# Scores of the first eight head pairs from whole fp32 operands, reads in natural order by TensorE, an earlier first load, and a re-fitted order

## The chip, the cores and the metric

One core of a Trainium2 chip runs the whole program: TensorE (PE, with its weight loads PEld), VectorE (DVE), ScalarE (ACT), GpSimd (POOL), and SyncE (SP), on whose queue all loads and stores of this kernel are issued. The metric is the device time of one execution in microseconds, the median of the runs.

## The reference, cut to what matters

```
q, k, v: (8, 12, 448, 64) fp32        w_in (768, 1024), w_spatial (448, 448), w_out (512, 768): float64
s    = cap * tanh(q k^T / sqrt(64) / cap)
attn = exp(s - max) / (sum(exp(s - max)) + 1e-9)
x    = attn v, heads side by side                  # (8, 448, 768)
h    = relu(x w_in); u, v = halves of h            # 512 columns each
v_n  = layernorm of v over its columns
out  = (u * (w_spatial v_n + b_spatial)) w_out     # (8, 448, 768)
```

The first four lines are called attention here, the rest the feed-forward part.

## The kernel before, in words

**Work units.** The 96 heads are worked in 48 pairs, six to a batch. A pair's keys are cut into four blocks of 112, worked two at a time (j = 0 and 1). For each j there is a score group on TensorE (into two buffers `ps_s`, one per block), two tanh on ScalarE (L545, reading `ps_s`, writing half of a tile `tp`), one exp over all of `tp` (L550), and a group of four matmuls that multiplies `tp` by the values (L559, into `ps_x`). Scores are transposed: keys lie on partitions, queries run along the free dimension. There are four `tp` tiles and two `ps_s` buffers, so j = 1 of a pair can't fill `ps_s` before the tanh of j = 0 has read it.

**Two precisions of matmul.** A matmul on plain fp32 operands (the values' group, and `ones` below) appears in the trace as two instructions. The scores are done in another way: `raw` (one buffer; 448 query and 448 key columns of both heads, one head on partitions 0 to 63, the other on 64 to 127) is rounded by ScalarE to `qh` (L310), VectorE subtracts to get the rest `ql` (L306), both in the type fp32r, and three terms qh·qh, ql·qh, qh·ql are accumulated: twelve single instructions for each j, which run in pairs (one head in each half of the array).

**Denominators.** The softmax's maximum is taken after exp. For each pair VectorE takes the larger of the two `tp` tiles (L580 over 1792 elements, L580 over 896), transposes blocks of 32 (L585), and reduces (L587) into `st`; a round trip through DRAM (`md`, `dt`) brings the partial results onto 32 partitions, where L616, L624 and L626 make the reciprocals, which go out (`rd`) and come back spread over the partitions (`rr`). The sum is taken by the same four VectorE instructions, except for the first `PE_SUMS` = 10 pairs: there TensorE multiplies `tp` by a block of ones (L599, eight matmuls in four column groups), ScalarE copies the rows to `sx` (L602), and DMAs bring them back (`td`, `dt`). POOL then multiplies (L645) and the result is split in two for the feed-forward part (`xg`).

**Natural order.** The host stores the queries permuted, query i·14+b at column b·32+i, because that is what the 32-blocks of the VectorE transpose want. Before the change the copies out of PSUM undo it: L564 and L602 read `ps_x` and `ps_acc` in a row and write with a step of 14 elements.

**Feed-forward part.** For each batch: u chains (L678 to L680), v chains (L700 to L705, whose rows are normalised by VectorE and POOL), gate chains (L769 to L774), output chains (L794 to L796), all in fp32r with three terms, chained in PSUM tiles `ps_acc`. Batch b's feed-forward matmuls are mixed with the next batch's pairs; the last batch's stand alone at the end. The weights come as float64 bits and are turned into `wi_h`, `wi_l` (12 pieces) and `wo_h`, `wo_l` (12 smaller pieces) once, in the first 180 us: POOL (L375), three VectorE operations (L379, L380, L382), a ScalarE cast, a VectorE subtraction (`wi_l`, L306).

**Order.** A planner (`Plan.order`) simulates the engines with a cost for each task and at each moment gives an engine the ready task with the smallest key. The keys come from `BND_KEY` and `BND_W_KEYS`; `TURN` and `STICK` are what it charges when TensorE changes between kinds of matmul, `MM`, `MMW` and `FF` its costs of matmuls. So these numbers change no instruction, only the order.

**Start.** Ahead of everything, `cap` is loaded and its bits decide a branch: here the `bounded` side is taken. Fourteen bf16 matmuls on zeros (`warm`) run while that is going on.

Of the kernel before, what the change touches and what calls it, by code (L numbers as in the profile page):

```python
# [167 lines left out]
HW, HH, XL, XF = 475, 650, 50, 4 / 360  # L170

# [68 lines left out]
def attn_moe(ctx, tc, bounded, shared, qk, v, qk2, v2, cap, w_in, w_sp, w_out, out):  # L240
# [278 lines left out]
    def pair_bnd(b, hp, xf, rr):  # L519
# [5 lines left out]
        t0 = add("S", HW, kk("ld"), lambda: nc.sync.dma_start(out=raw.t, in_=qk2[b, hp]), allocs=[raw], lat=XF * 128 * PW)  # L525
# [3 lines left out]
        t0 = add(e0, ct(e0, PW), kk("hi"), lambda: copy(e0, qh.t, raw.t), [t0], [raw], [qh], name="qh")  # L529
        t2 = add(e1, st2(e1, PW), kk("hi"), lambda: sub(e1, ql.t, raw.t, f(qh.t)), [t0], [raw, qh], [ql], name="ql")  # L530
        x, tps, exps, prev = Buf("x"), [], [], None
        for j in range(2):
            ps, tp = [Buf("s"), Buf("s")], Buf("tp")

            def scores(j=j, ps=ps):
                for i in range(2):
                    for n, (y, z) in enumerate(((qh, qh), (ql, qh), (qh, ql))):
                        for e in range(2):
                            r, c = slice(e * D, (e + 1) * D), S + (2 * j + i) * KB
                            nc.tensor.matmul(ps[i].t[:KB, e, :S], lhsT=y.t[r, c:c + KB], rhs=z.t[r, :S], start=(n == 0), stop=(n == 2))  # L540

            s = add("T", 6 * MM, kk("sc", j), scores, [t0, t2], [qh, ql, *ps], ps, name="sc", mode="R")
            for i in range(2):
                th = add("A", act(PW, 1), kk("th", j),
                         lambda i=i, ps=ps, tp=tp: nc.scalar.activation(  # L545
                             out=tp.t[:KB, i * PW:(i + 1) * PW].rearrange("p (e q) -> p e q", q=S), in_=ps[i].t[:KB, :, :S],
                             func=AF.Tanh, scale=ic[:KB]),
                         [s], [ps[i], tp], [tp] if i == 0 else [], name="tanh")
            ex = add("A", act_s(2 * PW, 1), kk("ex", j),
                     lambda tp=tp: nc.scalar.activation(out=tp.t[:KB], in_=tp.t[:KB], func=AF.Exp, scale=ca[:KB]), [th], [tp],  # L550
                     name="exp")
            tps.append(tp)
            exps.append(ex)

            def pv(j=j, tp=tp):
                for i in range(2):
                    for e in range(2):
                        c, o = 2 * j + i, (2 * i + e) * S
                        nc.tensor.matmul(x.t[e * D:(e + 1) * D, 0, :S], lhsT=vt.t[:KB, (2 * c + e) * D:(2 * c + e + 1) * D],  # L559
                                         rhs=tp.t[:KB, o:o + S], start=(c == 0), stop=(c == 3))  # L560
# [3 lines left out]
        z = add("A", act(S), kk("ev"), lambda: nc.scalar.copy(  # L564
            out=xf.t.rearrange("p (i b) -> p b i", b=QB), in_=x.t[:, 0, :S].rearrange("p (b i) -> p b i", i=32)), [prev], [x, xf],
            [xf], name="xev")

# [24 lines left out]
        if by_pe:  # L592
            acc, sx, td = Buf("acc"), Buf("sx"), Buf("td")

            def ones():
                for c in range(4):
                    for e in range(2):
                        o, i = e * D + c % 2 * 32, (c % 2 * 2 + e) * S
                        nc.tensor.matmul(acc.t[o:o + 32, 0, :S], lhsT=one[:KB], rhs=tps[c // 2].t[:KB, i:i + S], start=(c < 2), stop=(c > 1))  # L599
# [16 lines left out]
        d0 = add("V", 185, kk("dn"), lambda: nc.vector.reduce_max(  # L616
            out=sec(0), in_=grp()[:, :, :2 * QB].rearrange("p g b -> p b g"), axis=AX.X), [d], [dt], name="mred2")
# [201 lines left out]
def either(ctx: ExitStack, tc: tile.TileContext, *args):  # L819
# [5 lines left out]
    nc.sync.dma_start(out=capt[:, 0:1], in_=args[4].broadcast_to([128, 1]))
    with tc.tile_pool(name="wps", bufs=1, space=bass.MemoryType.PSUM) as wp, tc.tile_pool(name="warm", bufs=1) as ww:
        warm = ww.tile([128, WARM_N], mybir.dt.bfloat16, name="warm")
        nc.vector.memset(warm, 0.0)
# [2 lines left out]
            nc.tensor.matmul(ps, lhsT=warm[:, :128], rhs=warm, start=True, stop=True)  # L831
# [6 lines left out]
    nc.vector.memset(half, -0.5)  # L838
# [33 lines left out]
```

## Time and profile before

| | us |
|---|---|
| runs shown | 802.78 (median), 802.62, 805.45 |
| the profiled execution, its own time | 804.6 |
| its span, first to last instruction | 802.7 |
| PE / DVE / ACT / POOL busy | 763.1 / 707.3 / 575.5 / 228.6 |

A group's row gives, after the bar, busy time in us, the mean of one instruction in ns, and then the idle time of its engine just ahead of such instructions with what ended it. Busy time of PE counts a matmul up to its modelled end, so the distance from one start to the next, as the list in order of time shows it, is what a matmul costs in a stream.

### The profile page before, as it was taken

Reading aid. Unit: us, or ns where it says so; the run is one execution under the profiler, and the core shown is the slowest. Engines: PE = TensorE matmul, PEld = TensorE weight load, DVE = VectorE, ACT = ScalarE, POOL = GpSimd, SP = SyncE. Lnnn points to the kernel's source line nnn. Section 1 sums busy time; section 2 is a strip of 40 time slices with the busy share of each in tenths; the row PEclk is TensorE's granted clock in tenths of the full one; section 3 lists DMA queues with packets and bytes.
Section 4 is the critical chain, followed back from the end, with each engine's and each line's share of the span. In section 5 each row is a group of like instructions: output and inputs, shape, how many; then the busy total and the mean of one; then the engine's idle time right before and its main releaser. Section 6 shows DMA issues by size and latency. Waiting matters only on the chain.

```text
span 802.7 us, 11490 instructions
## 1 busy us (share of the span) xinstructions
PE 763.1 (95%) x4126; PEld 528.4 (66%) x4126; DVE 707.3 (88%) x934; ACT 575.5 (72%) x699; POOL 228.6 (28%) x179
## 2 busy tenths in 40 slices
PE   6878899979999999999999999999999999999997
PEld 2333456646776766667667677767677766767796
DVE  4979997899899997999999999999999999999340
ACT  4999877595777867687678876887677876874131
POOL 3131133341242103440143313330244212431150
PEclk8999999999999999999999999999999999999999
DMA  5544532433222332124221332223221332112102
GB/s 176 182 109 125 152 111 62 125 89 121 60 61 74 97 112 58 48 62 131 75 61 50 120 97 61 69 68 113 93 59 51 107 99 68 54 52 73 38 1 73
DMA packets 51254, 69.04 MB, mean 86 GB/s; under 512 B 23754, under 2 KB 36596, under 8 KB 51188
## 3 DMA queue, kind: packets, MB, share of 16 engines
q1 hardware_dynamic: 51188, 68.22, 28.7%
q8 instruction: 34, 0.56, 0.3%
q14 instruction: 32, 0.26, 0.1%
HBM read 55.70 MB, written 12.49 MB: 85 GB/s over the span
## 4 chain that ended last, share of the span: by engine, by line
PE 54%; DVE 24%; DMA 8%; ACT 7%; issue 5%; POOL 1%; SPq 1%; ACTq 0%; DVEq 0%; POOLq 0%
PE ps_x L559 10%; DVE red L580 10%; PE ps_s L540 9%; PE ps_acc L678 4%; PE ps_acc L679 4%; PE ps_acc L680 4%; DVE red L585 3%; DVE st L587 3%; ACT tp L545 2%; DMA dt<-md 2%; PE ps_acc L772 2%; ACT tp L550 2%; PE ps_acc L774 2%; PE ps_acc L773 2%; PE ps_acc L794 2%
## 5 line engine op out<-in xcount | busy, mean ns | idle before, releaser
L545 ACT ACTIVATE tp<-ps_s,capt 112x896 f32<-112x896 f32 x192 | 184.6, 1005 | 9.9 <-PE ps_s L540 8.9
L580 DVE TENSOR_TENSOR red<-tp 112x1792 f32<-112x1792 f32 x86 | 180.6, 2110 | 10.0 <-ACT tp L550 10.0
L550 ACT ACTIVATE tp<-tp,capt 112x1792 f32<-112x1792 f32 x96 | 172.4, 1796 | 2.3
L645 POOL TENSOR_TENSOR xf<-xf,rr 128x448 f32<-128x448 f32 x48 | 86.2, 1797 | 280.1 <-DMA rr<-rd 267.6
L559 PE MATMUL ps_x<-tp,v 112*64 112x448 f32 x768 | 157.2, 549 | 4.6 <-ACT tp L550 2.7
L559 PEld LDWEIGHTS ps_x<-tp,v 112*64 112x64 f32 x768 | 50.4, 137 | 87.2 <-issue 75.7
L580 DVE TENSOR_TENSOR red<-red 112x896 f32<-112x896 f32 x86 | 103.4, 1203 | 0.5
L585 DVE STREAM_TRANSPOSE red<-red 128x896 f32<-128x896 f32 x86 | 94.0, 1093 | 0.9
L587 DVE TENSOR_REDUCE st<-red 128x28 f32<-128x896 f32 x86 | 90.8, 1077 | 1.1
L540 PE MATMUL ps_s<-qh 64*112 64x448 f32 x384 | 81.2, 417 | 10.2 <-ACT tp L545 6.4
L540 PE MATMUL ps_s<-qh,ql 64*112 64x448 f32 x384 | 72.8, 372 | 6.6 <-DVE ql L306 6.5
L306 POOL TENSOR_TENSOR xg<-o,xg 128x448 fp32r<-128x448 f32 x32 | 46.1, 1443 | 107.4 <-ACT xg L310 107.4
L540 PEld LDWEIGHTS ps_s<-qh 64*112 64x112 f32 x384 | 34.0, 173 | 63.8 <-issue 28.1
L540 PE MATMUL ps_s<-ql,qh 64*112 64x448 f32 x384 | 72.2, 368 | 0.0
L678 PE MATMUL ps_acc<-xg,wi_h 128*128 128x448 f32 x186 | 69.7, 375 | 1.3 <-ACT xg L310 1.2
L794 PE MATMUL ps_acc<-xg,wo_h 128*128 128x448 f32 x184 | 69.3, 376 | 1.5 <-DVE o L779 1.2
L679 PE MATMUL ps_acc<-xg,wi_h 128*128 128x448 f32 x186 | 68.9, 371 | 1.1 <-DVE xg L306 1.1
L795 PE MATMUL ps_acc<-xg,wo_h 128*128 128x448 f32 x184 | 67.4, 366 | 1.6 <-POOL xg L306 1.6
L680 PE MATMUL ps_acc<-xg,wi_l 128*128 128x448 f32 x186 | 68.6, 369 | 0.0
L796 PE MATMUL ps_acc<-xg,wo_l 128*128 128x448 f32 x184 | 67.4, 366 | 0.0
L310 ACT CAST xg<-xf 128x448 fp32r<-128x448 f32 x96 | 36.5, 402 | 34.3 <-POOL xf L645 31.7
L306 DVE TENSOR_TENSOR ql<-raw,qh 128x896 fp32r<-128x896 f32 x48 | 53.3, 1111 | 7.2 <-ACT qh L310 7.2
(123 smaller groups left out, 1386.7 us busy)
## 6 DMA issues: line engine op xcount, KB each, us to landing
raw<-in_qk SPq DMA_DIRECT2D x48, 448.0 KB
v<-in_v SPq DMA_DIRECT2D x48, 224.0 KB
rr<-rd SPq DMA_DIRECT2D x96, 112.0 KB
out<-o SPq DMA_DIRECT2D x48, 224.0 KB
w<-in_w_in SPq DMA_DIRECT2D x12, 512.0 KB
xg<-in_w_out SPq DMA_DIRECT2D x12, 256.0 KB
md<-st SPq DMA_DIRECT2D x38, 28.0 KB
dt<-md SPq DMA_DIRECT2D x38, 28.0 KB
```

The costliest lines, as they stand in the source:

```text
L306: eng[e].tensor_tensor(o, a, b, op=ALU.subtract)
L540: nc.tensor.matmul(ps[i].t[:KB, e, :S], lhsT=y.t[r, c:c + KB], rhs=z.t[r, :S], start=(n == 0), stop=(n == 2))
L545: lambda i=i, ps=ps, tp=tp: nc.scalar.activation(out=tp.t[:KB, i * PW:(i + 1) * PW].rearrange("p (e q) -> p e q", q=S), in_=ps[i].t[:KB, : ...
L550: lambda tp=tp: nc.scalar.activation(out=tp.t[:KB], in_=tp.t[:KB], func=AF.Exp, scale=ca[:KB]), [th], [tp],
L559: nc.tensor.matmul(x.t[e * D:(e + 1) * D, 0, :S], lhsT=vt.t[:KB, (2 * c + e) * D:(2 * c + e + 1) * D], rhs=tp.t[:KB, o:o + S], start=(c == ...
L580: tt = lambda g, o_, i0, i1, op=op: eng[g].tensor_tensor(o_, i0, i1, op=op)
L585: d = add("V", dve(PW), kk(key), lambda r=r: nc.vector.transpose(out=blk(r.t[:, PW:]), in_=blk(r.t[:, :PW])), [d], [r], name="vtr")
L587: done.append(add("V", dve(PW), kk(key), lambda r=r, a=a, red=red: red(out=st.t[:, 2 * a * QB:2 * (a + 1) * QB], in_=blk(r.t[:, PW:]), axi ...
L645: m = add(E_X[0], st2(E_X[0], 448), k, lambda: eng[E_X[0]].tensor_tensor(xf.t, xf.t, rr.t, op=ALU.mult), deps, [xf, rr], name="xmul")
L678: nc.tensor.matmul(ps, lhsT=wi_h[:, c, fs], rhs=x[:, XH:], start=(c == 0), stop=False)
L679: nc.tensor.matmul(ps, lhsT=wi_h[:, c, fs], rhs=x[:, :S], start=False, stop=False)
L680: nc.tensor.matmul(ps, lhsT=wi_l[:, c, fs], rhs=x[:, XH:], start=False, stop=(c == NP - 1))
```

## The change

1. **Whole scores.** For the first `WHOLE` = 8 pairs no `qh` and `ql` are made; the scores are plain fp32 matmuls straight from `raw`.
2. **Natural order read by TensorE.** The values' group and `ones` read `tp` through `nat`: consecutive columns are 32 elements apart. The copies L564 and L602 become plain.
3. **First load and table ahead of the branch.** Pair 0's `raw` is a tile of its own (`raw0`, which later pairs use as the one `raw` buffer), loaded right behind `cap`; a tanh on one column makes ScalarE load its function table there too.
4. **Order.** New keys, weights' keys and costs; `PE_SUMS` 10 to 11.

```
-    TURN, STICK = 200.0, 0.74
+    TURN, STICK = 100.0, 0.68
-MM, MMW, TR = 207, 233, 109
+MM, MMW, TR = 204, 227, 109
-BND_KEY = dict(hi=-3.26, ld=-5.98, ...
+BND_KEY = dict(hi=-4.17, ld=-4.9, ...
...
-PE_SUMS = 10
+WHOLE = 8
+PE_SUMS = 11
...
+        if at:
+            t0 = add("S", HW, kk("ld"), lambda: nc.sync.dma_start(out=raw.t, in_=qk2[b, hp]), allocs=[raw], lat=XF * 128 * PW)
+        else:
+            t0 = add("S", 0, kk("ld") - 9, lambda: None, allocs=[raw])
...
+        whole = b * NP + hp < WHOLE
...
+        if not whole:
+            t0 = add(e0, ct(e0, PW), kk("hi"), lambda: copy(e0, qh.t, raw.t), [t0], [raw], [qh], name="qh")
+            t2 = add(e1, st2(e1, PW), kk("hi"), lambda: sub(e1, ql.t, raw.t, f(qh.t)), [t0], [raw, qh], [ql], name="ql")
+        terms = [(raw, raw)] if whole else [(qh, qh), (ql, qh), (qh, ql)]
...
+            if whole:
+                s = add("T", 2 * FF, kk("sc", j), scores, [t0], [raw, *ps], ps, name="sc", mode="R")
...
+            nat = lambda y: y.rearrange("p (b i) -> p i b", i=32)
...
-                                         rhs=tp.t[:KB, o:o + S], start=(c == 0), stop=(c == 3))
+                                         rhs=nat(tp.t[:KB, o:o + S]), start=(c == 0), stop=(c == 3))
...
-        z = add("A", act(S), kk("ev"), lambda: nc.scalar.copy(
-            out=xf.t.rearrange("p (i b) -> p b i", b=QB), in_=x.t[:, 0, :S].rearrange("p (b i) -> p b i", i=32)), [prev], [x, xf],
-            [xf], name="xev")
+        z = add("A", act(S), kk("ev"), lambda: nc.scalar.copy(out=xf.t, in_=x.t[:, 0, :S]), [prev], [x, xf], [xf], name="xev")
...
     nc.sync.dma_start(out=capt[:, 0:1], in_=args[4].broadcast_to([128, 1]))
+    raw0 = const.tile([128, PW], F32, name="raw0")
+    nc.sync.dma_start(out=raw0, in_=args[2][0, 0])
...
+    nc.scalar.activation(out=capt[:, 5:6], in_=half, func=AF.Tanh)
     bits = nc.values_load(capt[0:1, 1:2].bitcast(mybir.dt.int32), min_val=0, max_val=0x7FFFFFFF)
```

**What moves, on two engines.** Lines of the changed kernel are some 5 to 16 higher than before (L545 is L560, L559 is L576, L580 is L595, L306 is L311, L525 is L531).

SP at the start of the program, before (`capt` is cap's tile, `w_...` are pieces of w_in):

```order
L825 DMA capt<-in_cap 128x1
L834 TENSOR_LOAD capt
L840 COMPARE_AND_BRANCH
L525 DMA raw<-in_qk 128x896
L526 DMA v<-in_v 112x512 x2
L368 DMA w_187<-in_w_in 128x1024
L368 DMA w_189<-in_w_in 128x1024
```

and after:

```order
L838 DMA capt<-in_cap 128x1
L840 DMA raw_60<-in_qk 128x896
L851 TENSOR_LOAD capt
L856 COMPARE_AND_BRANCH
L534 DMA v<-in_v 112x512 x2
L373 DMA w_185<-in_w_in 128x1024
L373 DMA w_187<-in_w_in 128x1024
```

The first `raw` stands ahead of the branch, and the weights' loads move up one place.

DVE from the second `ql` of before to the third (`w_...` and `wy` are pieces of w_in on their way, `red_173` the tile of the first pair's reduction), before:

```order
L306 TENSOR_TENSOR ql<-raw,qh 128x896
L382 SCALAR_TENSOR_TENSOR wy<-w_191,wy 128x512
L306 TENSOR_TENSOR wi_l<-wy,wi_h 128x512
L379 TENSOR_SCALAR wy<-wy 128x512
L580 TENSOR_TENSOR red_173<-tp 112x1792
L380 SCALAR_TENSOR_TENSOR wy<-w_240,wy 128x512
L580 TENSOR_TENSOR red_173<-red_173 112x896
L306 TENSOR_TENSOR wi_l<-wy,wi_h 128x512
L585 STREAM_TRANSPOSE red_173<-red_173 128x896
L382 SCALAR_TENSOR_TENSOR wy<-w_240,wy 128x512
L587 TENSOR_REDUCE st<-red_173 128x28
L306 TENSOR_TENSOR ql<-raw,qh 128x896
```

and the stretch that stands there after:

```order
L311 TENSOR_TENSOR wi_l<-wy,wi_h 128x512
L387 SCALAR_TENSOR_TENSOR wy<-w_187,wy 128x512
L595 TENSOR_TENSOR red_173<-tp 112x1792
L311 TENSOR_TENSOR wi_l<-wy,wi_h 128x512
L595 TENSOR_TENSOR red_173<-red_173 112x896
L387 SCALAR_TENSOR_TENSOR wy<-w_195,wy 128x512
L600 STREAM_TRANSPOSE red_173<-red_173 128x896
L342 CAST ws_h<-wy 128x448
L602 TENSOR_REDUCE st<-red_173 128x28
L311 TENSOR_TENSOR wi_l<-wy,wi_h 128x512
L342 CAST ws_h<-wy 128x448
L595 TENSOR_TENSOR red_174<-tp 112x1792
```

No `ql` stands between the weights' pieces and the reductions any more, up to the ninth pair's. The last `wi_l` stands behind eight pairs' reductions (behind nine before), and two pieces of `wo_l` that stood ahead of it are now behind it.

SP around the load of the fifth pair's `raw`, after (`td_453` takes the third pair's sums from `sx`):

```order
L642 DMA rr_406<-rd_390 64x448 x2
L621 DMA dt_410<-td_375 32x2x14 x2
L627 DMA dt_410<-md_368 32x4x28
L534 DMA v_432<-in_v2 112x512
L618 DMA td_453<-sx_448 1x448
L531 DMA raw0_60<-in_qk2 128x896
L618 DMA td_453<-sx_448 1x448 x2
L640 DMA rd_472<-dt_410 32x2x14
```

The load of `raw` stands behind the first of the four DMAs that take the third pair's sums from `sx`; before the change the fifth pair's load stood behind those of the second pair.

More of the change, by code (lines that the diff above doesn't have):

```diff
@@ L216 @@
 BND_TAGS = {
-    "raw": (PW, F32, 1), "qh": (PW, F32R, 1), "sx": (448, F32, 1), "ql": (PW, F32R, 1), "v": (512, F32, 2), "tp": (2 * PW, F32, 4),
+    "qh": (PW, F32R, 1), "sx": (448, F32, 1), "ql": (PW, F32R, 1), "v": (512, F32, 2), "tp": (2 * PW, F32, 4),
     "xf": (448, F32, 2), "rr": (448, F32, 2), "st": (4 * QB, F32, 2), "dt": (20 * QB, F32, 2), **MOE_TAGS, "xg": (XW, F32R, 7),
@@ L224 @@
 ANY_W_KEYS = 2.0, 0.5, 8.0, 9.0, 1.0
-BND_KEY = dict(hi=-3.26, ld=-5.98, vld=-4.91, sc=-1.55, th=-0.93, ex=-1.87, pv=0.89, sm=0.69, mx=1.06, dn=-0.09,
-               ev=3.19, x=2.62, moe=0.79, span=12.63, step=0.24, mv=-1.51)
+BND_KEY = dict(hi=-4.17, ld=-4.9, vld=-1.5, sc=-1.65, th=1.93, ex=-1.09, pv=0.8, sm=0.23, mx=-0.07, dn=-0.32, ev=3.56,
+               x=2.65, moe=0.79, span=12.19, step=0.25, mv=-2.07)
 BND_V_FIRST = 1
 WARM, WARM_N = 14, 512
-BND_W_KEYS = 1.5, 1.89, 7.51, 13.76, 1.19
+BND_W_KEYS = 3.34, 2.17, 7.86, 13.43, 1.08
 E_SUM, E_RED = "VV", "VV"
-PE_SUMS = 10
+WHOLE = 8
+PE_SUMS = 11
 E_W = "PAV"
@@ L268, in make @@
             b.t = reds.pop(0)
+        elif b.tag == "raw" and bounded:
+            b.t = raw0
         elif b.tag == "md":
@@ L274, in make @@
             b.t = dr.tile([2 * S], F32, name="rd")
-    ic, ca, nca, half = shared
+    ic, ca, nca, half, raw0 = shared
     wi_h = const.tile([128, NP, DF], F32R, name="wi_h")
@@ L300, in attn_moe @@
     bufs["red"] = RED
+    if bounded:
+        bufs["raw"] = 1
     plan = Plan(bufs)
@@ L536, in scores @@
                 for i in range(2):
-                    for n, (y, z) in enumerate(((qh, qh), (ql, qh), (qh, ql))):
+                    for n, (y, z) in enumerate(terms):
                         for e in range(2):
                             r, c = slice(e * D, (e + 1) * D), S + (2 * j + i) * KB
-                            nc.tensor.matmul(ps[i].t[:KB, e, :S], lhsT=y.t[r, c:c + KB], rhs=z.t[r, :S], start=(n == 0), stop=(n == 2))
-            s = add("T", 6 * MM, kk("sc", j), scores, [t0, t2], [qh, ql, *ps], ps, name="sc", mode="R")
+                            nc.tensor.matmul(ps[i].t[:KB, e, :S], lhsT=y.t[r, c:c + KB], rhs=z.t[r, :S], start=(n == 0),
+                                             stop=(n == len(terms) - 1))
+            if whole:
+                s = add("T", 2 * FF, kk("sc", j), scores, [t0], [raw, *ps], ps, name="sc", mode="R")
+            else:
+                s = add("T", 6 * MM, kk("sc", j), scores, [t0, t2], [qh, ql, *ps], ps, name="sc", mode="R")
             for i in range(2):
@@ L598, in ones @@
                         o, i = e * D + c % 2 * 32, (c % 2 * 2 + e) * S
-                        nc.tensor.matmul(acc.t[o:o + 32, 0, :S], lhsT=one[:KB], rhs=tps[c // 2].t[:KB, i:i + S], start=(c < 2), stop=(c > 1))
+                        nc.tensor.matmul(acc.t[o:o + 32, 0, :S], lhsT=one[:KB], rhs=nat(tps[c // 2].t[:KB, i:i + S]), start=(c < 2), stop=(c > 1))
             sums = add("T", 2 * FF, kk("pv", 1) + 0.01, ones, exps, [u, w, acc], [acc], name="ones", mode="Q")
-            sums = add("A", 951, kk("ev"), lambda: nc.scalar.copy(
-                out=sx.t.rearrange("p (i b) -> p b i", b=QB), in_=acc.t[:, 0, :S].rearrange("p (b i) -> p b i", i=32)), [sums], [acc, sx],
-                [sx], name="sev")
+            sums = add("A", act(S), kk("ev"), lambda: nc.scalar.copy(out=sx.t, in_=acc.t[:, 0, :S]), [sums], [acc, sx], [sx], name="sev")
             sums = [add("S", HW, kk("dn"), lambda r=r: nc.sync.dma_start(out=td.t[r * S:(r + 1) * S], in_=sx.t[32 * r:32 * r + 1]), [sums],
@@ L823, in either @@
     const = ctx.enter_context(tc.tile_pool(name="shared", bufs=1))
-    capt = const.tile([128, 5], F32, name="capt")
+    capt = const.tile([128, 6], F32, name="capt")
     nc.sync.dma_start(out=capt[:, 0:1], in_=args[4].broadcast_to([128, 1]))
+    raw0 = const.tile([128, PW], F32, name="raw0")
+    nc.sync.dma_start(out=raw0, in_=args[2][0, 0])
     with tc.tile_pool(name="wps", bufs=1, space=bass.MemoryType.PSUM) as wp, tc.tile_pool(name="warm", bufs=1) as ww:
@@ L833, in either @@
     nc.vector.tensor_scalar(ca.bitcast(U32), capt[:, 0:1].bitcast(U32), 0x7FFFFFFF, None, op0=ALU.bitwise_and)
+    nc.vector.memset(half, -0.5)
+    nc.scalar.activation(out=capt[:, 5:6], in_=half, func=AF.Tanh)
     bits = nc.values_load(capt[0:1, 1:2].bitcast(mybir.dt.int32), min_val=0, max_val=0x7FFFFFFF)
@@ L837, in either @@
     nc.vector.tensor_scalar(nca, ca, -1.0, None, op0=ALU.mult)
-    nc.vector.memset(half, -0.5)
-    shared = ic, ca, nca, half
+    shared = ic, ca, nca, half, raw0
     with tc.If(bits <= CAP_BITS) as cmp:
```

13 lines of the change are left out of this document (5 added, 8 removed).

## Prediction

> **What bounds the kernel now.** I read the page's busy shares first, then a table of stretches, then the list in order of time for the start, then the groups.
>
> ```profile
> span 802.7 us, 11490 instructions
> ...
> PE   6878899979999999999999999999999999999997
> DVE  4979997899899997999999999999999999999340
> ACT  4999877595777867687678876887677876874131
> ```
>
> The digits are tenths of a slice of 20 us. After some 200 us PE is at 9 throughout; before that VectorE and ScalarE are the full ones and PE has holes. The stretches show how large these are (PE, PEld, DVE, ACT, POOL busy, then the granted clock).
>
> ```profile
> 0.00:13.00 13.00, 7.67 (x26) 3.45 (x26) 1.88 (x7) 2.85 (x3) 3.43 (x7) 0.83 0.54 159
> 13.00:50.00 37.00, 28.40 (x190) 11.95 (x186) 32.23 (x46) 36.22 (x39) 9.18 (x10) 0.96 0.56 171
> 50.00:85.00 35.00, 29.53 (x201) 13.14 (x199) 32.24 (x44) 32.71 (x35) 6.67 (x7) 0.96 0.40 108
> 85.00:121.30 36.30, 32.07 (x165) 19.17 (x162) 34.82 (x55) 29.83 (x38) 10.20 (x9) 0.95 0.46 137
> ...
> 150.00:180.00 30.00, 24.92 (x144) 16.47 (x142) 28.71 (x53) 21.70 (x32) 13.81 (x15) 1.00 0.42 122
> ...
> 270.00:360.00 90.00, 87.50 (x469) 59.43 (x468) 82.82 (x101) 64.45 (x79) 27.29 (x18) 1.00 0.27 80
> 360.00:451.00 91.00, 90.69 (x495) 65.07 (x494) 88.66 (x109) 70.19 (x85) 26.91 (x19) 1.00 0.27 81
> ```
>
> From 360 us on a batch takes 91 us and PE is busy in 90.69 of them: there only less work on PE would help, and VectorE with 88.66 is close behind. The holes are at the start. Up to 121.3 us PE is busy for 7.67 + 28.40 + 29.53 + 32.07 = 97.7 us, idle for 23.6; VectorE is busy for 101.2, idle for 20.1, of which 11.1 lie in the first 13 us; ScalarE for 101.6, idle for 19.7, with 10.1 in the first 13. I cut at 121.3 because there the last piece of `wi_l` begins. What VectorE does up to there:
>
> ```profile
> L580 DVE TENSOR_TENSOR red<-tp 112x1792 f32<-112x1792 f32 x9 | 18.1, 2014 | 2.9 <-ACT tp L550 2.9
> L306 DVE TENSOR_TENSOR ql<-raw,qh 128x896 fp32r<-128x896 f32 x10 | 10.9, 1091 | 6.3 <-ACT qh L310 6.3
> ...
> L306 DVE TENSOR_TENSOR wi_l<-wy,wi_h 128x512 fp32r<-128x512 f32 x12 | 8.2, 681 | 0.1
> ```
>
> Nine pairs' reductions, ten `ql`, all twelve pieces. From 13 to 121.3 us VectorE is busy for 99.3 of 108.3 us, so the weights come as fast as VectorE gets to them, and TensorE can't fill its holes with feed-forward work before they are there. That is the bound of this stage; ScalarE (98.8 of 108.3) is the next.
>
> **The start.**
>
> ```profile
> 1.17 5.19 PE L831 MATMUL wps<-warm 128*128 128x512 bf16 x14 [1.17 <-DVE capt L838]
> 4.48 0.35 SPq L525 DMA_DIRECT2D raw<-in_qk  x1
> 7.76 1.28 ACT L310 ACT_TABLE_LOAD   x1 [7.76 <-DMA raw<-in_qk]
> 9.06 0.94 ACT L310 CAST qh<-raw 128x896 fp32r<-128x896 f32 x1
> 10.09 0.71 PE L540 MATMUL ps_s<-qh 64*112 64x448 f32 x2 [3.73 <-ACT qh L310]
> 12.37 2.13 ACT L545 ACTIVATE tp<-ps_s,capt 112x896 f32<-112x896 f32 x2 [2.37 <-PE ps_s L540]
> 13.01 0.67 POOL L375 TENSOR_SCALAR wy<-w 128x512 f32<-128x512 f32 x1 [3.22 <-DMA w<-in_w_in]
> ```
>
> The rows give start and duration. `raw` is issued behind the branch at 4.48, the table load and the cast `qh` wait for it, the first score comes at 10.09 and the first tanh at 12.37; POOL's first piece of weights, which waits for its load, at 13.01. After the change `raw` leaves right behind `cap` (in the air while `warm` runs), so scores need only the end of `warm` at 1.17 + 5.19 = 6.36 and the branch: about 7.0 for the first score, some 8.2 for the first tanh, 4 us earlier. But VectorE is the bound, and it begins with weights. Their loads no longer stand behind 448 KB of `raw`. Between 4.48 and 13.01 went, by their shapes, raw with 448, two v with 224 each and w with 512 KB; without raw's share of 8.5 us it would be up to 448/1408 x 8.5 = 2.7 us less, at least 0 if something else sets 13.01. I take 1.5, in the middle. The table load (1.28 us) was on ScalarE's path ahead of `qh`; now it is ahead of the branch, hidden under `warm`.
>
> **Whole scores.** On VectorE eight `ql` go: 8 x 1.091 = 8.7 us, all ahead of the last `wi_l`. (The order puts one of nine reductions and two of the small `wo` pieces behind it; that is work moved, not saved.) On ScalarE eight `qh` go. On TensorE the price is read here:
>
> ```profile
> 21.70 1.72 PE L559 MATMUL ps_x<-tp,v 112*64 112x448 f32 x8 [0.50 <-ACT tp L550]
> 23.35 1.71 PE L599 MATMUL ps_acc<-tp,one 112*32 112x448 f32 x16
> 24.99 0.46 PE L540 MATMUL ps_s<-qh 64*112 64x448 f32 x2
> 25.28 0.37 PE L540 MATMUL ps_s<-qh,ql 64*112 64x448 f32 x2
> 25.49 0.37 PE L540 MATMUL ps_s<-ql,qh 64*112 64x448 f32 x2
> 25.69 0.38 PE L540 MATMUL ps_s<-qh 64*112 64x448 f32 x2
> ```
>
> A values' group of four fp32 matmuls (eight instructions, two abreast) lasts from 21.70 to 23.35: 1.65 us with the change of kind, so 1.50 of streaming in four steps of 0.376. The fp32r terms of the scores start 0.20 apart (25.28, 25.49, 25.69), six steps to a group: 1.20, or 1.29 with its longer first step. A whole group has four fp32 matmuls in the two halves of the array, hence I cost it like the values' group: 1.50, or 0.3 more, x 16 groups = 4.8 us. No row shows fp32 operands in two row halves; if the halves ran one after the other, a group would be 3.0 us, 28.8 us more in all; if they cost like the fp32r terms, nothing. I take 4.8, nearest to the rows for fp32. It falls in the stage in which PE is idle for 23.6 us; with 10.2 us less stage (sum below) 8.6 us of that cover are left.
>
> **Natural order.** The copies get shorter, and the reads of TensorE get steps of 32 elements.
>
> ```profile
> L550 ACT ACTIVATE tp<-tp,capt 112x1792 f32<-112x1792 f32 x96 | 172.4, 1796 | 2.3
> L564 ACT COPY xf<-ps_x 128x448 f32<-128x448 f32 x48 | 46.2, 962 | 8.1 <-DVE xg L306 5.8 <-PE ps_x L559 1.2 <-PE ps_acc L703 0.7
> L310 ACT CAST qh<-raw 128x896 fp32r<-128x896 f32 x48 | 45.6, 950 | 8.1 <-PE ps_s L540 7.6 <-DMA raw<-in_qk 0.4
> L310 ACT COPY o<-ps_acc 128x448 f32<-128x448 f32 x46 | 24.4, 535 | 45.7 <-DMA out<-o 24.3 <-PE ps_acc L796 18.0 <-PE ps_s L540 1.8
> L616 DVE TENSOR_REDUCE dt<-dt 32x28 f32<-32x112 f32 x48 | 16.0, 334 | 8.4 <-DMA dt<-md 8.2
> L587 DVE TENSOR_REDUCE st<-red 128x28 f32<-128x896 f32 x86 | 90.8, 1077 | 1.1
> ```
>
> The copy into `xf`, which writes with a step, took 962 ns (`sx` is of the same form), a plain copy of 128x448 out of PSUM (`o`) 535: 0.43 us less x 59 copies on ScalarE. Together with `qh` that is 8 x 0.95 + 16 x 0.43 = 14.5 us less in the first stage, so ScalarE will not be what holds VectorE up. Later ScalarE is at 3/4 and the gain is only that of waits:
>
> ```profile
> L559 PE MATMUL ps_x<-tp,v 112*64 112x448 f32 x768 | 157.2, 549 | 4.6 <-ACT tp L550 2.7 <-ACT xf L564 1.8
> L540 PE MATMUL ps_s<-qh,ql 64*112 64x448 f32 x384 | 72.8, 372 | 6.6 <-DVE ql L306 6.5
> ```
>
> The first row ends with PE's waits for the copy `xf`, 1.8 us; I take 1.0 (0 to 1.8). The second row's 6.5 us of waits for `ql` end where no `ql` is made.
>
> What strided reads cost TensorE no row shows. There are 96 x 4 + 11 x 4 = 428 fp32 steps that read `tp`. The lower end is 0 (nothing makes a longer step a gain). The upper is the ratio that ScalarE pays, 962/535 = 1.80: 0.30 us a step, 129 us in all. VectorE's strided reduction (334 ns for 112 elements, against 1077 for 896 in a row) says that reads pay, too. Which is nearer? An fp32 step spends 376 ns on 448 columns, 0.84 ns each; an fp32r step 0.45. So an fp32 column already has twice the time of one that TensorE can take at its full rate, while ScalarE and VectorE pay a factor of about two against their own full rate. I take 0. [...]
>
> **One more pair with `ones`.** VectorE loses four instructions, where PE is the bound; PE gets one group: +1.6 (23.35 to 24.99).
>
> **The single `raw` buffer.** TensorE now holds it until the j = 1 scores are done, and the load that follows takes
>
> ```profile
> 11.21 5.39 DMA raw<-in_qk
> ```
>
> 5.39 us among the weights' loads. From the end of one pair's first two tanh, ScalarE has exp, two tanh, exp (1.80 + 2.13 + 1.80, the pair of tanh as at 12.37) and two plain copies with two or three casts, by the rows above an estimated 2.5 us, ahead of the next pair's: 8.2 us. The load's path is about 1.0 for the rest of the scores, 0.35 to issue, 5.39, 0.75 for one block, and 0.4 of hand-overs: 7.9. So it is just hidden, at no cost; each us by which SP issues it late shows.
>
> **The order.** Kinds of matmul change 213 times instead of 218, at about 0.1 us each (25.28 - 24.99 = 0.29 against 0.20): -0.5. In the steady part the groups stand in the same pattern. What the new order can do to the holes at 150 to 180 (5.1 us idle) and 270 to 360 (2.5) is anything from -7.6 to about as much more; I take 0. The planner's changed costs are no instructions.
>
> **The sum.** VectorE's lead at the last `wi_l`: 8.7 + 1.5 = 10.2. From there PE is the bound, and its work is as before but for +1.6, -0.5 and -1.0. So -10.2 + 1.6 - 0.5 - 1.0 = -10.1 us: span 802.7 to 792.6. The profiled execution took 804.6, 1.9 more than its span, and the median of the runs is 802.78, 1.8 below it; on the median I get 792.7, rounded 792.5. Half a per cent, about 4 us, is what a measurement here can tell from no change.
>
> **The rivals.**
> 1. *Strided reads cost TensorE.* For: the ScalarE and VectorE rows above. Against: the fp32 step's slack. [...] At ScalarE's ratio the time is 792.5 + 129 = 921; at a third of that 835. It decides from 10.1/428 = 24 ns a step: beyond that the kernel is slower than before.
> 2. *The load of `raw` becomes the wait.* For: SP has the fifth pair's load behind `td`, which waits for ScalarE's copy `sx`, and ScalarE's own chain has only 0.3 us of slack. Against: fewer bytes before it. If SP's queue holds it for some 1.7 us in each of seven pairs, the 10 us are gone: about 802, no change.
> 3. *Row halves don't run abreast in fp32.* Of 28.8 us instead of 4.8, 24.0 more, 8.6 are covered: 792.5 + 15.4 = 808, slower. Against: fp32r row halves and fp32 column halves both do.
>
> **Chances.** My forecast 0.75, with its own range 780 to 799. Below: the order's -7.6, the loads' further -1.2, the waits' further -0.8, and some 3 of the 9.0 us that VectorE idles from 13 to 121 us. Above: the order's loss, up to where no change begins. Rival 1 0.12, rival 2 0.10, rival 3 0.03. So faster 0.75, within half a per cent 0.10, slower 0.15. The range of 780 to 803 takes in rival 2 and leaves out the slower cases and a little below.
>
> **What would show it.** Right: whole-score groups about 1.5 us apart, values' groups still four steps of 0.376, `xf` copies near 535 ns, first tanh near 8.2 us, the last `wi_l` near 110 or, by the moved work, some 8 us earlier, the steady batches still 91 us, PE idle before 121 us down from 23.6 to about 10. Wrong: values' steps above 0.40 (rival 1), PE or ScalarE waiting for DMA `raw` at each of the first eight pairs (rival 2), whole groups of 3 us (rival 3), or new waits of PE after 150 us.

## The result and the profile after

The changed kernel takes 947.86 us (median, 947.01 to 949.24) against 803.62 for the kernel before on the same chip: a ratio of 1.178, with an interval of 1.175 to 1.181. The profiled execution took 949.24 us, with a span of 947.4. The prediction said 792.5. What was given as its first rival came, at more than its price.

The head of the page after, with the busy shares, the digits of three engines, and the chain that ended last:

```profile
span 947.4 us, 11388 instructions
PE 933.1 (98%) x4078; PEld 532.2 (56%) x4078; DVE 684.8 (72%) x922; ACT 554.5 (59%) x693; POOL 206.8 (22%) x179
...
PE   8998999999999999999999999999999999999997
...
DVE  4677556667977887787877787778787877787540
ACT  4666565566574656665675565846566665746132
...
PE 97%; DMA 2%; DVE 0%; issue 0%; ACT 0%; SPq 0%; POOL 0%; ACTq 0%; DVEq 0%
```

PE's digits are 9 nearly from the first slice to the last, its busy time rose from 763.1 to 933.1 us, and VectorE and ScalarE, full at the start before, now stand at 4 to 7 in the first ten slices. TensorE alone is the bound. The stretches say the same (PE, PEld, DVE, ACT, POOL busy):

```profile
85.00:121.30 36.30, 36.30 (x135) 9.79 (x134) 19.49 (x31) 21.04 (x25) 3.96 (x4) 1.00 0.31 89
...
360.00:451.00 91.00, 91.00 (x414) 55.16 (x413) 72.37 (x90) 55.77 (x68) 20.74 (x17) 1.00 0.22 64
```

In the stretch ahead of 121.3 us, where PE had 4.2 us of holes before, it has none. From 360 to 451 us it is busy as before, but 414 matmuls fit into the stretch where 495 did. The groups that show why (busy time, mean of one, idle time ahead):

```profile
L576 PE MATMUL ps_x<-tp,v 112*64 112x448 f32 x768 | 309.0, 956 | 1.6 <-ACT tp L565 0.8 <-ACT xf L581 0.8
L614 PE MATMUL ps_acc<-tp,one 112*32 112x448 f32 x176 | 43.6, 1093 | 0.0
L551 PE MATMUL ps_s<-raw 64*112 64x448 f32 x128 | 31.3, 610 | 6.5 <-DMA raw<-in_qk 3.7 <-ACT wi_h L315 2.2 <-ACT tp L560 0.4
L581 ACT COPY xf<-ps_x 128x448 f32<-128x448 f32 x48 | 25.5, 532 | 54.5 <-PE ps_x L576 47.2 <-issue 4.8 <-DVE xg L311 2.5
```

L576 is the values' group (L559 before): the same 768 instructions, 309.0 us instead of 157.2. L581, the copy into `xf`, did fall from 962 ns to 532. In order of time, PE:

```profile
20.67 3.25 PE L576 MATMUL ps_x<-tp,v 112*64 112x448 f32 x8
23.85 4.06 PE L614 MATMUL ps_acc<-tp,one 112*32 112x448 f32 x16
27.84 1.76 PE L551 MATMUL ps_s<-raw 64*112 64x448 f32 x8
29.54 3.28 PE L576 MATMUL ps_x<-tp,v 112*64 112x448 f32 x8
```

A values' group of four steps lasts from 20.67 to 23.85, 3.18 us; before it was 1.65 (21.70 to 23.35). A `ones` group takes 3.99 instead of 1.64. The whole scores, which read `raw` in a row, take 1.70, just as costed. So only the two kinds of matmul that read `tp` with a step of 32 elements are dear. (The word has two uses here: a step of so many *elements* is the distance in the tile between two columns read in succession; a values' or `ones` step is the *time* from the start of one instruction, or of those that run abreast, to the next within a group.) Over all groups the median of a values' step is 0.773 us instead of 0.376; a `ones` step takes about 0.99, a quarter of its group. A whole batch now takes 109.5 us from its first values' group to the next batch's, instead of 91.

### The profile page after: what moved, and what is told of

Read it like the earlier page. It is cut to its first block, busy times and chain, and to the rows that moved or that the text cites. A ratio compares the mean times of both kernels' runs of the same rounds, so it can differ in the third digit from the quotient of the medians.

```text
span 947.4 us, 11388 instructions
## 1 busy us (share of the span) xinstructions
PE 933.1 (98%) x4078; PEld 532.2 (56%) x4078; DVE 684.8 (72%) x922; ACT 554.5 (59%) x693; POOL 206.8 (22%) x179
## 4 chain that ended last, share of the span: by engine, by line
PE 97%; DMA 2%; DVE 0%; issue 0%; ACT 0%; SPq 0%; POOL 0%; ACTq 0%; DVEq 0%
PE ps_x L576 32%; PE ps_s L551 15%; PE ps_acc L614 5%; PE ps_acc L807 4%; PE ps_acc L691 4%; PE ps_acc L692 4%; PE ps_acc L693 4%; PE ps_acc L809 4%; PE ps_acc L808 4%; PE ps_acc L716 3%; PE ps_acc L717 3%; PE ps_acc L718 3%; PE ps_acc L785 2%; PE ps_acc L787 2%; PE ps_acc L786 2%; PE ps_acc L713 1%
## 5 line engine op out<-in xcount | busy, mean ns | idle before, releaser
L576 PE MATMUL ps_x<-tp,v 112*64 112x448 f32 x768 | 309.0, 956 | 1.6 <-ACT tp L565 0.8
L560 ACT ACTIVATE tp<-ps_s,capt 112x896 f32<-112x896 f32 x192 | 185.4, 1009 | 65.2 <-PE ps_s L551 64.6
L595 DVE TENSOR_TENSOR red<-tp 112x1792 f32<-112x1792 f32 x85 | 177.1, 2100 | 25.9 <-ACT tp L565 25.6
L576 PEld LDWEIGHTS ps_x<-tp,v 112*64 112x64 f32 x768 | 55.7, 149 | 194.2 <-issue 184.1
L658 POOL TENSOR_TENSOR xf<-xf,rr 128x448 f32<-128x448 f32 x48 | 62.0, 1291 | 351.5 <-DMA rr<-rd 350.1
L595 DVE TENSOR_TENSOR red<-red 112x896 f32<-112x896 f32 x85 | 100.7, 1185 | 0.4
L311 DVE TENSOR_TENSOR ql<-raw,qh 128x896 fp32r<-128x896 f32 x40 | 43.6, 1090 | 76.7 <-ACT qh L315 72.7
L602 DVE TENSOR_REDUCE st<-red 128x28 f32<-128x896 f32 x85 | 91.0, 1070 | 1.0
L315 ACT CAST qh<-raw 128x896 fp32r<-128x896 f32 x40 | 37.8, 946 | 89.4 <-PE ps_s L551 89.4
L311 POOL TENSOR_TENSOR xg<-o,xg 128x448 fp32r<-128x448 f32 x32 | 48.9, 1541 | 156.6 <-ACT xg L315 156.6
L551 PE MATMUL ps_s<-qh 64*112 64x448 f32 x320 | 66.3, 409 | 0.0
L551 PEld LDWEIGHTS ps_s<-qh 64*112 64x112 f32 x320 | 27.9, 170 | 66.0 <-issue 57.4
L551 PE MATMUL ps_s<-ql,qh 64*112 64x448 f32 x320 | 59.2, 362 | 0.0
L551 PE MATMUL ps_s<-qh,ql 64*112 64x448 f32 x320 | 59.0, 362 | 0.0
```

What stands on the lines that cost most here:

```text
L560: lambda i=i, ps=ps, tp=tp: nc.scalar.activation(out=tp.t[:KB, i * PW:(i + 1) * PW].rearrange("p (e q) -> p e q", q=S), in_=ps[i].t[:KB, : ...
L595: tt = lambda g, o_, i0, i1, op=op: eng[g].tensor_tensor(o_, i0, i1, op=op)
```

## The experiments

**E1: the change without the strided reads of TensorE.** The values' group and `ones` read in a row again, ScalarE's two copies write with a step again; each engine's order is that of the changed kernel.

```
-                                         rhs=nat(tp.t[:KB, o:o + S]), start=(c == 0), stop=(c == 3))
+                                         rhs=tp.t[:KB, o:o + S], start=(c == 0), stop=(c == 3))
...
-        z = add("A", act(S), kk("ev"), lambda: nc.scalar.copy(out=xf.t, in_=x.t[:, 0, :S]), [prev], [x, xf], [xf], name="xev")
+        z = add("A", act(S), kk("ev"), lambda: nc.scalar.copy(
+            out=xf.t.rearrange("p (i b) -> p b i", b=QB), in_=x.t[:, 0, :S].rearrange("p (b i) -> p b i", i=32)), [prev], [x, xf],
+            [xf], name="xev")
...
```

> The changed kernel with its natural-order reads alone undone: TensorE reads tp in a row again, ScalarE's copies write with the step again, and every engine's order is that of the changed kernel. If the strided reads cost TensorE everything that was lost (a values' step of 0.773 us against 0.376 over 384 steps is 152 us, and 44 steps of ones at about 1.0 against 0.376 another 27), the time is 948 - 180 + the idle time of PE that comes back, and the rest of the change shows what it is worth: by the forecast 793, between 780 and 803. If the new order or the whole scores cost time too, it ends above 807.

Measured: 790.3 us (789.12 to 792.08), 0.984 of before (0.981 to 0.987). The head of its page, stretches and groups:

```profile
span 788.7 us, 11388 instructions
PE 761.1 (96%) x4078; PEld 524.4 (66%) x4078; DVE 672.7 (85%) x922; ACT 570.8 (72%) x693; POOL 214.1 (27%) x179
...
0.00:13.00 13.00, 9.91 (x38) 3.39 (x38) 0.79 (x6) 6.97 (x7) 3.86 (x8) 1.00 0.63 180
13.00:50.00 37.00, 26.84 (x136) 8.38 (x136) 32.41 (x49) 27.86 (x29) 11.30 (x11) 0.91 0.44 137
50.00:85.00 35.00, 29.95 (x155) 11.02 (x156) 28.87 (x42) 31.78 (x37) 10.13 (x9) 0.90 0.63 181
85.00:121.30 36.30, 35.72 (x188) 21.16 (x187) 30.28 (x50) 27.42 (x34) 9.70 (x8) 1.00 0.30 94
121.30:150.00 28.70, 28.62 (x172) 19.00 (x175) 24.20 (x52) 20.78 (x29) 10.61 (x14) 1.00 0.36 107
150.00:180.00 30.00, 28.69 (x170) 18.72 (x164) 24.67 (x41) 25.45 (x35) 11.40 (x8) 1.00 0.37 115
...
270.00:360.00 90.00, 90.00 (x494) 65.27 (x492) 83.64 (x107) 68.47 (x84) 23.12 (x18) 1.00 0.27 81
...
L576 PE MATMUL ps_x<-tp,v 112*64 112x448 f32 x768 | 159.6, 555 | 2.5 <-ACT xf L581 1.6 <-ACT tp L565 0.8
L616 PE MATMUL ps_acc<-tp,one 112*32 112x448 f32 x176 | 18.8, 545 | 0.0
L551 PE MATMUL ps_s<-raw 64*112 64x448 f32 x128 | 31.3, 608 | 14.7 <-DMA raw<-in_qk 14.2 <-ACT tp L560 0.4
```

One edit moves the span by 947.4 - 788.7 = 158.7 us. Of PE's 172.0 us more busy time (933.1 - 761.1), the values give 149.4 (309.0 - 159.6) and `ones` 24.8 (43.6 - 18.8). PE's idle time went down from 27.6 to 14.3, the 13.3 us between 172.0 and 158.7. So the whole of the loss is the strided reading, and everything else in the change together gains.

**E2: the kernel before with the strided reads alone** (E1's edits the other way, on the kernel before).

> The kernel before with the natural-order reads alone, its own keys and qh, ql for all pairs. If the strided reads are the cause by themselves: 384 steps 0.397 longer and 40 steps 0.62 longer are 177 us more work on PE, of which at most the 20 to 40 us that PE idled before are covered, so 940 to 980. If the loss needs the new order or the whole scores as well, below 900.

Measured, in one run: 955.67 us, span 953.8; the values' group is busy for 309.4 us, a `ones` instruction takes 1103 ns. The cost is there with the old order and the old scores.

**E3: a ladder of steps.** In the kernel before, batches 0 to 7 read the moving operand of scores and values with another step each:

```
+STEPS = 1, 1, 2, 4, 8, 16, 32, 1
...
+        step = lambda y: y.rearrange("p (b i) -> p i b", i=STEPS[b]) if STEPS[b] > 1 else y
...
+                                         rhs=step(tp.t[:KB, o:o + S]), start=(c == 0), stop=(c == 3))
```

> The kernel before, in which the moving operand of the scores (fp32r) and of the values' group (fp32) is read with a step of 1, 1, 2, 4, 8, 16, 32, 1 elements in batches 0 to 7 (queries come out permuted, so the output is not the reference's). What is read from it is the distance between steps of the two kinds in each batch. [...]

Measured: the values' groups, one row for each batch's stretch, steps 1, 1, 2, 4, 8, 16, 32, 1 from top to bottom (busy time is that of 47 or 48 steps):

```profile
L561 PE MATMUL ps_x<-tp,v 112*64 112x448 f32 x94 | 21.2, 585 | 3.8 <-ACT tp L552 3.7
L561 PE MATMUL ps_x<-tp,v 112*64 112x448 f32 x96 | 22.8, 617 | 0.9 <-ACT xf L566 0.9
L561 PE MATMUL ps_x<-tp,v 112*64 112x448 f32 x94 | 20.1, 563 | 0.0
L561 PE MATMUL ps_x<-tp,v 112*64 112x448 f32 x96 | 39.2, 968 | 0.0
L561 PE MATMUL ps_x<-tp,v 112*64 112x448 f32 x94 | 38.9, 984 | 0.0
L561 PE MATMUL ps_x<-tp,v 112*64 112x448 f32 x94 | 36.6, 932 | 0.0
L561 PE MATMUL ps_x<-tp,v 112*64 112x448 f32 x96 | 38.6, 958 | 0.0
L561 PE MATMUL ps_x<-tp,v 112*64 112x448 f32 x96 | 19.4, 546 | 0.0
```

The medians from start to start are 376, 376, 394, 787, 804, 751, 776, 376 ns. It is a switch, not a slope: a step of two elements is nearly free (394 against 376), from four elements on it costs 2.0 to 2.1 times as much, and a longer step costs about the same. The fp32r scores of the same run, two rows each from the batches with steps 1, 2 and 16:

```profile
145.47 0.36 PE L542 MATMUL ps_s<-qh,ql 64*112 64x448 f32 x2
145.67 0.37 PE L542 MATMUL ps_s<-ql,qh 64*112 64x448 f32 x2
...
237.42 0.58 PE L542 MATMUL ps_s<-ql,qh 64*112 64x448 f32 x2
237.82 0.58 PE L542 MATMUL ps_s<-qh 64*112 64x448 f32 x2
...
583.65 0.56 PE L542 MATMUL ps_s<-ql,qh 64*112 64x448 f32 x2
584.03 0.56 PE L542 MATMUL ps_s<-qh 64*112 64x448 f32 x2
```

They start 0.20, 0.40 and 0.38 us apart. In fp32r the doubling is there at a step of two already (0.40 against 0.20), where fp32 pays 18 ns. Why is open.

**E8: is it the sharing of the array?** All 48 pairs have whole scores, the values' matmuls run one at a time instead of two abreast, and the ladder of steps is on both.

```
-WHOLE = 8
+WHOLE = 48
...
-                        nc.tensor.matmul(x.t[e * D:(e + 1) * D, 0, :S], lhsT=vt.t[:KB, (2 * c + e) * D:(2 * c + e + 1) * D],
-                                         rhs=nat(tp.t[:KB, o:o + S]), start=(c == 0), stop=(c == 3))
+                        nc.tensor.matmul(x.t[:D, 0, :S], lhsT=vt.t[:KB, (2 * c + e) * D:(2 * c + e + 1) * D],
+                                         rhs=step(tp.t[:KB, o:o + S]), start=(c == 0 and e == 0), stop=(c == 3 and e == 1))
```

> The first experiment's kernel with whole scores for all 48 pairs, both heads' values' groups accumulated into the same 64 columns of the array (so one matmul at a time; the output is not the reference's), and the ladder of steps 1, 1, 2, 4, 8, 16, 32, 1 in batches 0 to 7 for both. In the first ladder the fp32 step of two matmuls that read the same partitions was 0.376, 0.394, 0.787, 0.804, 0.751, 0.776 us at steps 1, 2, 4, 8, 16, 32, and the fp32r step of two on different partitions 0.203, 0.397, 0.404, 0.379, 0.380, 0.382. If the slowing belongs to the reading of one stream, single fp32 matmuls and fp32 scores in two row halves go from 0.376 to about 0.77 at step 4 and more, too. If it comes from two streams on the same partitions sharing the reads, single matmuls and row halves stay at 0.376 to 0.40 at all steps. For step 2, where fp32 was free and fp32r was not: if that is the operand type's doing, the fp32 scores are free at 2; if it is the row halves' doing, they are at 0.77 already at 2.

Measured, in one run: 1172.73 us. Values, steps 2 and 4, then whole scores, steps 2 and 4:

```profile
L576 PE MATMUL ps_x<-tp,v 112*64 112x448 f32 x95 | 38.7, 558 | 0.0
L576 PE MATMUL ps_x<-tp,v 112*64 112x448 f32 x96 | 76.7, 966 | 0.0
...
L553 PE MATMUL ps_s<-raw 64*112 64x448 f32 x95 | 22.0, 575 | 0.0
L553 PE MATMUL ps_s<-raw 64*112 64x448 f32 x96 | 40.6, 976 | 0.0
```

A single step, one instruction on the array, takes, over the ladder, 376, 376, 393, 787, 803, 750, 755, 376 ns, the same as two abreast in E3, and two in the row halves the same again (medians 376, 394, 789, 804, 751, 756 ns at steps 1 to 32). So the doubling belongs to the stream of one instruction, and two streams don't hinder each other; only the four abreast of `ones`, in the changed kernel, cost more, 0.99 against 0.376. E8 also answers one half of what E3 left: fp32 in the row halves is nearly free at a step of two, so it is not the row halves that make fp32r pay there. The type of the operand is the difference that is left.

**E4: the natural order made elsewhere.** E1 with ScalarE's copy in a row, and POOL's multiplication reading `xf` with a step of 32:

```
+            three = lambda y, p: y.rearrange(p, i=32)
+            m = add(E_X[0], st2(E_X[0], 448), k, lambda: eng[E_X[0]].tensor_tensor(
+                three(rr.t, "p (i b) -> p i b"), three(xf.t, "p (b i) -> p i b"), three(rr.t, "p (i b) -> p i b"), op=ALU.mult),
```

> The first experiment's kernel (reads in a row) with the unpermuting moved from ScalarE's copy out of ps_x to POOL's multiplication: POOL reads xf with a step of 32 elements and writes in a row into rr. ScalarE gets 48 x 0.43 = 20 us shorter; POOL has about 70 per cent idle time. If POOL's strided read costs it nothing, it takes 1.2 us as before and the time is 0 to 3 us below the first experiment's (the 0.8 to 1.8 us that PE waited for xf copies). If POOL pays a factor of two as ScalarE does, 1.0 us more stands in each pair's chain, and the time is the same or up to 2 us longer.

Measured: 793.65 us (792.81 to 796.53), 0.989 of before (0.986 to 0.992). Its row for the multiplication:

```profile
L662 POOL TENSOR_TENSOR rr<-xf,rr 128x448 f32<-128x448 f32 x48 | 81.5, 1699 | 282.4 <-DMA rr<-rd 245.1 <-DVE red L595 26.6 <-ACT tp L565 10.1
```

ScalarE has 46.2 - 25.4 = 20.8 us less to do, POOL 13.2 more (81.5 against 68.3 in E1), and the time is 3.4 us longer than E1's 790.3, outside both forecasts (0 to 3 us shorter, or up to 2 longer). That is near the least that can be told here; what is clear is that ScalarE's gain doesn't show in the time, and why it doesn't is open. The mean of POOL's instruction differs between kernels that read alike (1797 ns in the kernel before, 1423 in E1, both in a row), so it says little about the step. Its median is 1418 ns and its least 1356; in a row they are 1157 and 1132 in the changed kernel, 1222 and 1129 in the kernel before. By the least, the step costs POOL about a fifth, not the factor of two that was the second case.

**E5, E6, E7: the rest of the change, one part out at a time**, each on E1. E5 has no whole scores:

```
-WHOLE = 8
+WHOLE = 0
```

> The first experiment's kernel (reads in a row, 790.3 us) with no whole scores: qh and ql for all 48 pairs again. By the forecast's ledger VectorE gets 8 ql of 1.09 us back ahead of the last wi_l while the 4.8 us less on PE lie under its idle time: 799. If ScalarE's 8 qh count as well, up to 803. If the new order alone made the gain, 790.

E6 has the keys, costs and `PE_SUMS` of before (all but four of the planner's costs for small VectorE tasks, which stay as in the change):

```
-BND_KEY = dict(hi=-4.17, ld=-4.9, ...
+BND_KEY = dict(hi=-3.26, ld=-5.98, ...
...
-PE_SUMS = 11
+PE_SUMS = 10
```

> The first experiment's kernel with all numbers of the order as they were before (keys, weights' keys, TURN, STICK, costs, PE_SUMS = 10), whole scores and early load kept. By the forecast the order is worth 0 and the eleventh pair with ones costs 1.6, so 789 to 791. The span of the first experiment came out 4 us below the forecast, and the holes at 150 to 180 and 270 to 360 us are smaller there; if that is the order's doing, 794 to 797. If the old keys, which want ql early and v later, do not suit whole scores at all, above 800.

E7 has the first load and the table load behind the branch again:

```
-    nc.sync.dma_start(out=raw0, in_=args[2][0, 0])
...
-    nc.scalar.activation(out=capt[:, 5:6], in_=half, func=AF.Tanh)
```

> The first experiment's kernel with the first load of raw and the function table behind the branch again. By the forecast the early load is worth 1.5 us on VectorE: 792. The first experiment's trace has POOL's first piece of weights at 12.57 us against 13.01, so 0.4 us: 790.7. If the 5.5 us by which the first tanh came earlier (6.91 against 12.37) carry through, 795.

Measured: E5 810.15 us, 1.008 of before (1.005 to 1.011); E6 813.77, 1.015 (1.009 to 1.022); E7 790.29, 0.982 (0.978 to 0.986). E5 missed all three values that were expected; E6 went by its last case, above 800, not by the forecast's 789 to 791. Two stretches of E5, then two of E6:

```profile
50.00:85.00 35.00, 27.28 (x169) 12.08 (x171) 31.77 (x46) 33.15 (x38) 4.82 (x4) 0.90 0.38 108
...
121.30:150.00 28.70, 20.93 (x74) 15.02 (x76) 23.16 (x46) 8.65 (x14) 9.24 (x10) 0.76 0.26 81
```

```profile
50.00:85.00 35.00, 24.34 (x130) 7.55 (x130) 33.99 (x53) 30.40 (x36) 8.10 (x8) 0.90 0.47 137
...
270.00:360.00 90.00, 84.11 (x450) 59.92 (x450) 86.24 (x106) 63.60 (x77) 27.49 (x18) 0.96 0.25 74
```

With the new order and no whole scores (E5) VectorE has the eight `ql` to do again; the last `wi_l` comes at 141.1 us instead of 107.2, and PE has 7.8 us of holes from 121.3 to 150 where E1 has 0.1. With whole scores and the old order (E6) PE is idle for 10.7 us from 50 to 85 (5.1 in E1) and for 5.9 from 270 to 360 (none in E1). Each half alone is slower than before, by 0.8 and 1.5 per cent, the two together are 13 us faster: the gain can't be shared out between them.

E7 is as fast as E1, though its start is later. The first tanh and POOL's first piece of the weights, in E1 and then in E7:

```profile
6.91 1.90 ACT L560 ACTIVATE tp<-ps_s,capt 112x896 f32<-112x896 f32 x2 [4.69 <-PE ps_s L551]
...
12.57 0.64 POOL L380 TENSOR_SCALAR wy<-w 128x512 f32<-128x512 f32 x1 [3.46 <-DMA w<-in_w_in]
```

```profile
10.52 1.91 ACT L557 ACTIVATE tp<-ps_s,capt 112x896 f32<-112x896 f32 x2
...
12.49 0.67 POOL L380 TENSOR_SCALAR wy<-w 128x512 f32<-128x512 f32 x1 [2.67 <-DMA w<-in_w_in]
```

The tanh is 3.6 us earlier in E1, the weights aren't earlier at all (13.01 in the kernel before, 12.57 and 12.49 here).

**E9: the wait for `raw`.** E1's L551 row has PE waiting 14.2 us for the load of `raw`, in five places. E9-two loads whole pairs' `raw` in turn into two tiles, E9-three into three:

```
-            raw, vt = Buf("raw"), Buf("v")
+            raw, vt = Buf(("raw", "qh")[hp % 2] if whole else "raw"), Buf("v")
```

> E1 with the raw tiles of the first eight pairs loaded alternately into the raw tile and the qh tile (which nothing else uses there), so that the load of one pair's raw need not wait for the scores of the pair before. In E1 PE waits 14.2 us in five places for DMA raw in this stage. Theory A (these waits lie beside VectorE's bound, as the prediction said of the load: just hidden, at no cost): PE's waits for raw fall below 5 us but the last wi_l stays within 2 us of E1's 107.2 us and the time is 788 to 792. Theory B (the waits are on the path that sets the end): the stage shortens by up to those 14 us, the last wi_l comes before 103 us and the time is 778 to 786.

> As E9-two, with three tiles in turn (raw, qh, ql), so that the loads of the second and third pair stand ahead of pieces of the weights. Theory A: PE waits less still for raw, but each load ahead of a weights' piece pushes that piece back by about 1.5 us, and since the weights bound the stage the time is 789 to 794, no better than E9-two. Theory B: as for E9-two, 778 to 786.

Measured: E9-two 795.21 us (792.92 to 797.5), 0.990 of before (0.987 to 0.993); E9-three 794.2, 0.990 (0.987 to 0.993). Both theories missed E9-two: no gain, but not the same either; E9-three is just outside of what theory A gave, and for another reason than its 1.5 us a piece. E9-two's row for the pairs in the `raw` tile, and two stretches:

```profile
L553 PE MATMUL ps_s<-raw 64*112 64x448 f32 x64 | 15.6, 602 | 1.9 <-ACT tp L562 1.8
...
85.00:121.30 36.30, 28.63 (x151) 16.47 (x151) 30.55 (x47) 26.82 (x32) 12.32 (x10) 0.91 0.41 124
121.30:150.00 28.70, 25.39 (x117) 18.28 (x119) 22.51 (x51) 15.12 (x24) 10.77 (x13) 0.94 0.11 30
```

The waits are gone and PE is busy for 62.2 us from 13 to 85 us (56.8 in E1); then it has holes of 7.7 and 3.3 us, as the last `wi_l` begins at 130.4 us instead of 107.2 (127.5 in E9-three). The pairs, no longer held by their load, run ahead: ten pairs' reductions stand on VectorE ahead of the last `wi_l`, eight pairs' in E1. One reading is that the wait for `raw` had been holding the pairs to a pace that suited the weights; it is argued, not shown, for the planner made a new order for the two tiles, and its share and the load's weren't told apart. E7 speaks to the same question without a second tile:

```profile
L548 PE MATMUL ps_s<-raw 64*112 64x448 f32 x128 | 31.1, 607 | 10.9 <-DMA raw<-in_qk 6.5 <-ACT tp L562 2.6 <-ACT tp L557 1.7
```

It waits 6.5 us for `raw` where E1 waits 14.2, and takes the same time. E1 (and E7, equal to it) stays the fastest version that was run.

## Why the prediction was wrong, and where it was right

- **The step that failed** is "What strided reads cost TensorE no row shows ... I take 0". It measured 0.397 us a values' step (0.773 - 0.376) and about 0.61 a `ones` step: 384 x 0.397 + 44 x 0.61 = 179 us counted by steps, 174 by busy time. The upper end given, 0.30 a step from ScalarE's ratio, was too small as well, and so was the rival's 921.
- **The reason that the prediction gave for it** was that an fp32 column, with 0.84 ns, has twice the time of an fp32r column (0.45 ns), whose rate it took for TensorE's full one. That slack wasn't there. In E3, beyond a step of two elements, an fp32 step costs 0.75 to 0.80 us, twice the 0.38 to 0.40 of fp32r, as it is about twice in a row (0.376 against 0.20): both kinds doubled, and the longer time of an fp32 column took up none of it. At a step of two the two are alike (0.394 against 0.40). What fills the longer time of an fp32 column no run shows; the doubling itself is measured.
- **The weighing**: the two rows for strided access (ScalarE 1.80, VectorE's small reduction) spoke one way, and a single argument from a rate the other way; it got 0.75. The reduction spoke more weakly than it was read: VectorE's L624, on 28 elements in a row, takes 194 ns, so much of the reduction's 334 needn't be the step. The point of decision, 24 ns a step, was right and small against every priced row.
- **The rest of the sum** came out near, but not by its own working. Without the strided reads the prediction goes from 792.6 to 793.6 of span (its 1.0 for the copy goes with them); E1 has 788.7, 14.0 less than before where 9.1 were forecast. By busy and idle time of PE: 2.0 less work, 12.0 less idle. The idle time lies elsewhere than forecast: up to 121.3 us it is 18.9 (23.6 before, about 10 forecast), from 150 to 180 1.3 instead of 5.1, from 270 to 360 none instead of 2.5. The prediction had put these last two down as what the order could do, "anything from -7.6 to about as much more", and taken 0.
- **The lead at the last `wi_l`**, 10.2 us, was the main term: what VectorE gains up to there was to come off the time, one for one. In E1 it looks so: the last `wi_l` begins at 107.2 instead of 121.3, within the forecast, and the span is 14.0 shorter. The other versions don't follow:

| | last `wi_l` begins, us | span, us |
|---|---|---|
| before | 121.3 | 802.7 |
| E1 | 107.2 | 788.7 |
| E6 (old order) | 112.1 | 810.6 |
| E9-two | 130.4 | 793.7 |
| E5 (no whole scores) | 141.1 | 807.4 |

E6 reaches it 9.2 us earlier than before and ends 7.9 later; E9-two reaches it 9.1 later and ends 9.0 earlier. So this step isn't borne out as a mechanism, and that E1 comes within 5 us of the forecast is in part luck. What sets the gain, beyond that it needs whole scores and new order together, is open.

- **Whole scores**: 1.70 us a group with its change of kind (1.65 for fp32 values before): right, and rival 3 is out. The 8.7 us on VectorE and the order's 0 are not separate terms (E5, E6).
- **The early load**: 1.5 us were forecast, 0 measured (E7). The first tanh came at 8.35 us in the changed kernel, as forecast, and at 6.91 in E1; the first weights came no earlier with the early load than without.
- **`xf` copies**: 532 ns, as forecast; their gain on PE can't be seen (E4).
- **Rival 2**: PE does wait for `raw` in E1, 14.2 us in five places. That is more than "just hidden", and yet E7 with less than half of it takes the same time and E9 without it takes 4 to 5 us more (with another order). So no run shows it as a loss. In the changed kernel the wait is 3.7 us, in two places.
- **The steady batches** keep their 91 us in E1 (PE busy for all of 270 to 360); in the changed kernel TensorE's 48 values' steps a batch alone add 48 x 0.397 = 19.1, and the batch takes 18.5 more (109.5).

## What to carry to other kernels

Don't let TensorE read a moving operand with a step (here of four elements or more in fp32, 0.75 to 0.80 us against 0.376, or of two or more in fp32r, 0.38 to 0.40 against 0.20) to spare another engine a reordering, above all where TensorE is the bound: there each ns comes out of the end, here 8 x 0.397 = 3.2 us a pair on an engine that is full, against 0.43 us a pair on one that had a quarter free. A slow rate is not slack until a row shows it: where the nearest rows of other engines all pay, give the price of the nearest row, not nothing. And an order fitted to a kernel belongs to that kernel: change one of the two alone, and the time can get worse, as in E5 and E6.

## What was not expected of the hardware

- The price of a step is a switch: fp32 394 ns at two elements, 787 at four, 804, 751 and 755 to 776 at 8, 16 and 32. 16 is cheaper than 8 in both ladders; why isn't known.
- fp32r pays about the whole of it at two elements: 0.40 us against 0.20.
- Four strided streams abreast (`ones`, 0.99 us) cost more than two or one (0.75 to 0.80), while one and two cost the same.
- POOL's multiplication, reading one operand with a step of 32, took 1418 ns (median, E4) against 1157 in a row (the changed kernel); ScalarE's copy with a stepped write cost 1.8 times a plain one (962 ns before, 532 after). Of these three TensorE pays the most, 2.0 to 2.1 times in fp32 from a step of four on.
